# Attention ahead of two gated networks on one core: outer blocks' edge keys side by side, sums on GpSimd, another order of steps

## The chip, the cores and the metric

One core of a Trainium2 chip runs the whole program in one launch. The metric is the device time of an execution in microseconds (us). TensorE is called PE (its weight loads PEld), VectorE DVE, ScalarE ACT, GpSimd POOL, and SyncE, on whose queue nearly all transfers are issued, SP.

## What is computed

```python
def _attn_ref(q_l, k_l, v_l, q_g, k_g, v_g):      # B, H, Sl, D = 4, 8, 512, 64; Sg = 32
    k_all = np.concatenate([k_g, k_l], axis=2)
    v_all = np.concatenate([v_g, v_l], axis=2)
    out_g = np.matmul(sm(scale * np.matmul(q_g, k_all.transpose(0, 1, 3, 2))), v_all)
    mask = np.abs(pos[:, None] - pos[None, :]) <= 32
    s_ll = np.where(mask, scale * np.matmul(q_l, k_l.transpose(0, 1, 3, 2)), -1e9)
    s_lg = scale * np.matmul(q_l, k_g.transpose(0, 1, 3, 2))
    out_l = np.matmul(sm(np.concatenate([s_lg, s_ll], axis=-1)), v_all)
    return np.concatenate([out_g, out_l], axis=2)

x = attention, as (4 * 544, 512)
x = (sigmoid(x @ w_gate) * (x @ w_val)) @ w_out        # 512 -> 1536 -> 512
h = x @ w_in                                           # 512 -> 2048
g = (a0 + a1 h + a2 h^2 + a3 h^3) / (1 + |b0| |h| + |b1| h^2 + 1e-6)
out = g @ w_out2                                       # 2048 -> 512
```

All is float32; `sm` is a softmax over the keys, with 1e-9 added to the sum.

## The kernel before

Attention runs as 16 units, each a batch entry and a pair of heads (`j` = 0, 1, one in each half of the partitions). A unit's 512 local queries are four blocks `c` of 128. A block sees only its own 128 keys and up to 96 edge keys: the 32 global ones and 32 on either side; the first and last block (c = 0 and 3) have one neighbour only, so 64 edge keys and 192 in all where the inner ones have 224 (`KEYS`). For each block and head the steps are:

- `s_mm(u, half)`: scores of two blocks on PE into one of two score buffers (`pairs`); `s_max`: mask, scale and maximum on DVE, into the tile `p`; `s_exp`: exponential and its row sum on ACT; `s_add`, `s_rec`: the sum gets its 1e-9 (a reduction over two columns) and is inverted, on DVE; `s_norm`: the normalisation on POOL, both heads in one instruction.
- `t_mm(u, c)`: four PE transposes (own keys of both heads, then 128 columns with the edge keys of either head) into one of four `banks` of PSUM; `t_out`: one copy of 512 columns out of it, on DVE for c = 0 and 2, on ACT for 1 and 3.
- `v_own`, `v_edge`: products with own and edge values on PE; `x_hi` (ACT), `x_lo` (DVE): the result as two parts; `x_g`, `x_out`: its share of the global queries.

The global queries of two units go together: `g_mm` (PE), `g_max` (DVE), `g_exp` (ACT), `g_rec` (DVE), `g_norm` (POOL), `g_turn` (PE), `e_own` (DVE), `e_edge` (ACT). In between, `w_mag`, `w_bits`, `w_add`, `w_hi` and `w_lo` prepare the first weights of the gated network, which starts with `first(0, 0)`, line 723, when all units are done.

Every engine works through its own list in order. The lists come from the table `STEPS`: each step has a place for unit 0, unit 1, the even and odd units in between, and units 14 and 15; the place of a middle unit is its number plus the table's value, and all steps are issued in the order of these places. The buffers (`Slots`) are taken and given back in that same order: two score buffers, four banks, four tiles of keys, three of queries, values and probabilities. A step that takes a buffer waits for the last use before it.

Of the kernel before, what the change touches and what calls it, by code (L numbers as in the profile page):

```python
# [8 lines left out]
F32 = mybir.dt.float32  # L9
# [27 lines left out]
def tile_of(tok):  # L37
# [19 lines left out]
    ('g_load', (-193.6, None, 4.1758, None, -6.26303, None)),  # L57
# [11 lines left out]
    ('s_norm', 0, 1, (1.15869, 3.05293, 7.0023, 6.88967, 6.8235, 8.84887)),
    ('s_add', 0, (-4.78283, 1.74976, 6.09143, 6.12871, 6.18832, 6.08334)),  # L70
    ('s_rec', 0, (-4.63935, 2.74797, 6.2835, 6.31798, 6.21174, 6.47475)),
    ('s_mm', 1, (-37.43525, -11.09496, 5.07416, 4.48179, 5.14953, 5.5168)),
    ('s_max', 1, 0, (-32.36454, -4.31373, 5.37653, 4.99397, 5.32926, 5.67216)),
    ('s_exp', 1, 0, (-28.29228, 5.29168, 5.84691, 6.27648, 5.63018, 6.75453)),
    ('s_norm', 1, 0, (-19.32734, 6.416, 6.34497, 7.13507, 9.01965, 27.97716)),
    ('s_max', 1, 1, (-26.61698, -6.53723, 5.38946, 5.68801, 5.52636, 5.70039)),
    ('s_exp', 1, 1, (-26.56671, 5.18384, 5.81313, 6.30095, 5.93787, 5.86118)),
    ('s_norm', 1, 1, (1.44586, 6.17569, 7.31762, 7.11427, 7.91441, 11.00704)),
    ('s_add', 1, (-20.31348, 5.90938, 6.14497, 6.64992, 6.09973, 7.27147)),
    ('s_rec', 1, (-19.82663, 6.09145, 6.28248, 6.68668, 6.10739, 8.17753)),  # L80
    ('g_mm', (-27.40611, None, 4.501, None, 4.54575, None)),
    ('g_max', (-26.24706, None, 4.71585, None, 4.64024, None)),
    ('g_exp', (-24.76355, None, 4.94489, None, 5.02262, None)),
    ('g_rec', (-14.86346, None, 5.73461, None, 6.29334, None)),
    ('g_norm', (-14.83861, None, 6.20628, None, 6.92266, None)),
    ('g_turn', (-6.44609, None, 6.70996, None, 6.93773, None)),
    ('e_own', (1.49794, -1.68988, 6.8847, 5.74138, 8.26861, 6.11579)),
    ('e_edge', (2.81072, 2.58086, 7.08973, 6.25701, 8.30143, 6.79597)),
    ('t_mm', 0, (0.8243, 5.9286, 7.28143, 7.79149, 9.41117, 40.10613)),
    ('t_out', 0, (2.43049, 6.10843, 7.68441, 7.94095, 11.87654, 41.58592)),  # L90
    ('v_own', 0, (4.15643, 6.25318, 7.70991, 8.55565, 394.83877, 414.41785)),
    ('v_edge', 0, (4.99735, 6.3075, 7.87462, 8.61583, 395.97761, 414.51208)),
    ('t_mm', 1, (2.22876, 5.75977, 7.19455, 7.68987, 14.15807, 11.38739)),
    ('t_out', 1, (5.28033, 5.92209, 7.49688, 7.80584, 23.59935, 19.86153)),
    ('v_own', 1, (5.89053, 6.83402, 8.18053, 8.61706, 434.20982, 415.84308)),
    ('v_edge', 1, (6.05524, 6.85992, 8.19946, 8.79119, 437.33562, 419.33359)),
    ('t_mm', 2, (-8.43225, 7.73408, 7.32894, 7.95716, 10.57072, 42.59335)),
    ('t_out', 2, (2.42448, 7.97099, 7.75793, 7.99656, 15.45124, 414.50625)),
    ('v_own', 2, (4.32497, 8.69969, 8.00172, 9.00748, 396.7707, 424.89989)),
    ('v_edge', 2, (4.86799, 8.73029, 8.1423, 9.33108, 397.12023, 426.50916)),  # L100
    ('t_mm', 3, (3.98898, 6.97862, 7.32925, 7.65514, 10.38176, 13.58618)),
    ('t_out', 3, (5.43741, 7.38094, 7.82717, 7.77506, 14.15911, 29.43003)),
# [67 lines left out]
def attention(ctx, tc, ident, xh, xl, ins, other):  # L170
# [33 lines left out]
    for t in wn:  # L204
        nc.gpsimd.memset(t[0 : 128 - EDGE], 0.0)
# [1196 lines left out]
```

## Time and profile before

| what | value |
|---|---|
| median of 3 runs | 899.43 us (898.97 to 900.34) |
| profiled execution | 898.83 us, its span 896.9 us |
| PE busy | 889.3 us, 99% of the span |
| DVE, ACT, POOL busy | 750.1, 576.2, 576.0 us |
| granted TensorE clock | 1.0 of full speed in the whole span |
| attention stage | to 114.58 us, when the first gated matmul starts |

Busy time counts an instruction from its start to its end. Matmuls are pipelined and their ends are modelled, so several short matmuls in a row overlap in the profile; how far apart they start tells more than how long one is.

### The profile page before, as it was taken

The numbers are of one execution on the slowest core, as the hardware profiler recorded it, in microseconds if no ns is written. First come the engines' busy times: TensorE is split into PE (matmuls) and PEld (weight loads), VectorE is DVE, ScalarE is ACT, GpSimd is POOL, SyncE is SP. The second block draws the span as 40 slices with busy tenths as digits, with TensorE's granted clock in tenths as the row PEclk, the third lists the DMA queues.
The fourth block names the chain that finished last, engine by engine and source line by source line (L and its number), as shares of the span: only waits on it lengthen the run. The fifth ranks groups of instructions, "written<-read, shape, count | busy, mean of one in ns | idle before, by whom it ended". The sixth has DMA issues, their size and how long they took to land.

```text
span 896.9 us, 13592 instructions
## 1 busy us (share of the span) xinstructions
PE 889.3 (99%) x4592; PEld 737.3 (82%) x4592; DVE 750.1 (84%) x1300; ACT 576.2 (64%) x1161; POOL 576.0 (64%) x470
## 2 busy tenths in 40 slices
PE   8999999999999999999999999999999999999997
PEld 6788988888888888888888888888888888888886
DVE  6999967988889888766868699987788899888886
ACT  6999865445554344354444488777777787777773
POOL 5768765767767485476767767544555676666564
PEclk9999999999999999999999999999999999999999
DMA  9775274767667686999998960022001300110112
GB/s 307 242 219 170 83 280 169 267 227 252 232 236 262 231 300 217 322 339 321 341 352 331 360 213 1 1 94 94 1 1 51 114 24 1 43 51 1 48 59 94
DMA packets 60372, 155.87 MB, mean 174 GB/s; under 512 B 7056, under 2 KB 8720, under 8 KB 60304
## 3 DMA queue, kind: packets, MB, share of 16 engines
q1 hardware_dynamic: 60208, 154.89, 49.7%
q8 instruction: 36, 0.59, 0.3%
q14 instruction: 32, 0.26, 0.1%
q10 hardware_dynamic: 96, 0.13, 0.1%
HBM read 102.83 MB, written 52.17 MB: 173 GB/s over the span
## 4 chain that ended last, share of the span: by engine, by line
PE 87%; DVE 7%; ACT 1%; POOL 1%; issue 0%; POOLq 0%; ACTq 0%
PE rp L1255 6%; PE rp L1257 6%; PE rp L1256 6%; PE rp L725 5%; PE rp L723 5%; PE rp L724 5%; PE p L844 4%; PE p L842 4%; PE p L843 4%; PE pg L723 3%; PE pg L724 3%; PE pg L725 3%; PE pv L723 3%; PE pv L724 3%; PE pv L725 3%; PE pair L265 2%
## 5 line engine op out<-in xcount | busy, mean ns | idle before, releaser
L1172 POOL TENSOR_TENSOR v<-v,u 128x512 f32<-128x512 f32 x68 | 93.4, 1374 | 105.6 <-ACT v L1168 103.4
L1226 POOL TENSOR_TENSOR rgl<-t,rgh 128x512 fp32r<-128x512 f32 x64 | 89.1, 1393 | 40.6 <-POOL v L1172 17.3
L1255 PE MATMUL rp<-wide,rgh 128*128 128x512 f32 x204 | 79.5, 390 | 0.6 <-DVE racc L1276 0.6
L1257 PE MATMUL rp<-wide,rgl 128*128 128x512 f32 x204 | 79.4, 389 | 0.0
L1256 PE MATMUL rp<-wide,rgh 128*128 128x512 f32 x204 | 79.4, 389 | 0.0
L1165 ACT ACTIVATE u<-rp 128x512 f32<-128x512 f32 x68 | 40.5, 596 | 60.2 <-PE rp L725 57.3
L1180 DVE TENSOR_TENSOR t<-rp,t 128x512 f32<-128x512 f32 x68 | 46.7, 687 | 38.7 <-ACT t L1176 37.6
L723 PE MATMUL rp<-yh,wide 128*128 128x512 f32 x192 | 75.0, 391 | 0.0
L1205 DVE SCALAR_TENSOR_TENSOR t<-t,co,v 128x512 f32<-128x512 f32 x68 | 72.9, 1072 | 2.4
L770 ACT CAST gh<-t 128x512 fp32r<-128x512 f32 x38 | 23.6, 620 | 79.7 <-DVE t L763 76.0
L725 PE MATMUL rp<-yh,wide 128*128 128x512 f32 x192 | 74.7, 389 | 0.0
L724 PE MATMUL rp<-yl,wide 128*128 128x512 f32 x192 | 74.7, 389 | 0.0
L1201 DVE SCALAR_TENSOR_TENSOR v<-v,u 128x512 f32<-128x512 f32 x68 | 73.8, 1085 | 0.0
L301 POOL TENSOR_TENSOR p<-p,r 128x384 f32<-128x384 f32 (+1 forms) x64 | 55.4, 889 | 28.4 <-DVE r L295 13.9
L1197 DVE SCALAR_TENSOR_TENSOR v<-v,u 128x512 f32<-128x512 f32 x68 | 61.7, 908 | 1.1 <-ACT u L1193 1.1
L285 ACT ACTIVATE p<-p,mx 128x224 f32<-128x224 f32 (+1 forms) x128 | 58.5, 467 | 6.1 <-DVE mx L277 6.1
L856 DVE TENSOR_TENSOR gacc<-p,gacc 128x512 f32<-128x512 f32 x80 | 51.2, 680 | 10.1 <-PE p L844 10.1
L1168 ACT ACTIVATE v<-u,co 128x512 f32<-128x512 f32 x68 | 55.6, 817 | 2.3
L775 DVE TENSOR_TENSOR gl<-t,gh 128x512 fp32r<-128x512 f32 x38 | 37.4, 985 | 23.1 <-ACT gh L770 23.0
L1189 ACT ACTIVATE u<-v,co 128x512 f32<-128x512 f32 x68 | 49.2, 724 | 6.2 <-POOL v L1172 6.0
L1176 ACT ACTIVATE t<-rp,co 128x512 f32<-128x512 f32 x68 | 51.7, 761 | 0.0
L1214 ACT CAST rgh<-t 128x512 fp32r<-128x512 f32 x64 | 39.1, 611 | 18.0 <-DVE t L1205 18.0
(724 smaller groups left out, 2913.1 us busy)
## 6 DMA issues: line engine op xcount, KB each, us to landing
raw1gv<-in_w_gate_val SPq DMA_DIRECT2D x24, 512.0 KB, 4.2
raw2in<-in_w_in SPq DMA_DIRECT2D x16, 512.0 KB, 5.0
raw2out<-in_w_out SPq DMA_DIRECT2D x16, 512.0 KB, 5.0
kn<-in_k_l SPq DMA_DIRECT2D x15, 448.0 KB, 5.5
raw1out<-in_w_out SPq DMA_DIRECT2D x12, 512.0 KB, 4.2
vn<-in_v_l SPq DMA_DIRECT2D x16, 256.0 KB, 3.2
out<-racc SPq DMA_DIRECT2D x16, 256.0 KB, 2.0
qn<-in_q_l SPq DMA_DIRECT2D x15, 256.0 KB, 4.5
```

Source lines behind the costliest of these rows:

```text
L285: nc.scalar.activation(p, p, AF.Exp, bias=s["mx", half][:, n : n + 1], scale=-1.0, accum_out=s["sm", half][:, n, 0:1])
L723: nc.tensor.matmul(ps, wh, mh[:, k], start=k == 0, stop=False)
L724: nc.tensor.matmul(ps, wh, ml[:, k], start=False, stop=False)
L725: nc.tensor.matmul(ps, wl, mh[:, k], start=False, stop=k == 3)
L1172: nc.gpsimd.tensor_tensor(s["v"], s["v"], s["u"], ALU.mult)
L1197: nc.vector.scalar_tensor_tensor(s["v"], s["v"], Q_CONST, s["u"], ALU.add, ALU.mult)
L1201: nc.vector.scalar_tensor_tensor(s["v"], s["v"], 2.0, s["u"], ALU.subtract, ALU.mult)
L1205: nc.vector.scalar_tensor_tensor(s["t1"], s["t1"], a0, s["v"], ALU.add, ALU.mult)
L1226: nc.gpsimd.tensor_tensor(s["gl"], s["t1"], s["gh"].bitcast(F32), ALU.subtract)
L1255: nc.tensor.matmul(ps, gh[:, w], wh, start=k == 0, stop=False)
L1256: nc.tensor.matmul(ps, gh[:, w], wl, start=False, stop=False)
L1257: nc.tensor.matmul(ps, gl[:, w], wh, start=False, stop=k == G - 1)
```

## The change

In the outer blocks (c = 0 and 3) the two heads' probabilities lie side by side: own keys of head 0, the 64 edge keys of head 0, the 64 of head 1, own keys of head 1. One transpose of the 128 columns in the middle turns the edge keys of both heads, so `t_mm` issues three transposes there and `t_out` copies 384 columns. The edge values of an outer block are laid out in 128 rows, with zeros where the other head's keys stand, so `v_edge` has the same count of matmuls; edge values are loaded as 128 rows for all blocks. Keys lie in 960 columns per unit for 896, with the edge keys of an outer block on both sides of its own keys, and `g_mm` reads the own keys in two pieces of 256 columns. `g_norm` copies the 32 global columns to a second place, and `e_edge` becomes two copies of 64 partitions. `s_add` becomes an addition on POOL. The fills of the edge values and of unused probabilities go; the mask has a third part. All places of the table change from unit 1 on (unit 0 keeps its own).

```diff
+OUTER = (0, NBLK - 1)
+KAT = (0, 256, 256 + WIN, 256 + 2 * WIN, 512 + 2 * WIN)
 STEPS = [
...
-    ('load', 'k', (None, -181.26379, 4.10399, 2.93904, -7.29458, 3.04983)),
-    ('load', 'q', (None, -40.52201, 4.43, 2.15593, 4.42898, -1.01145)),
-    ('load', 'v', (3.92294, -7.4328, 4.44095, 7.56662, 9.81241, 4.88656)),
-    ('load', 'w', (-28.52292, 6.10594, 6.86833, 6.60856, 7.04185, 5.77992)),
+    ('load', 'k', (None, -61.63139, 3.4381, 2.24976, 3.62724, -4.25923)),
+    ('load', 'q', (None, -28.06102, 4.04664, 3.68304, -0.91483, 3.9796)),
+    ('load', 'v', (3.92294, 5.78863, 6.77615, 6.6405, 6.54417, 8.82375)),
+    ('load', 'w', (-28.52292, 5.13391, 6.65689, 7.96598, 332.79805, 9.10943)),
...
-    ('x_out', (397.6786, 9.48477, 15.22727, 12.74181, 508.4924, 477.88016)),
+    ('x_out', (397.6786, 369.83157, 485.83533, 10.26943, 485.83433, 495.48873)),
...
-    kept = dict(kn=slots(one, "kn", 4, [128, NBLK, WIN]), qn=slots(one, "qn", 3, [128, NBLK, 128]),
+    kept = dict(kn=slots(one, "kn", 4, [128, KAT[-1]]), qn=slots(one, "qn", 3, [128, NBLK, 128]),
...
+    def probs(u, c, j):
+        if c in OUTER:
+            return st[u]["p"][:, c].rearrange("p j k -> p (j k)")[:, j * KEYS[c] : (j + 1) * KEYS[c]]
+        return st[u]["p"][:, c, j]
...
-    for t in wn:
-        nc.gpsimd.memset(t[0 : 128 - EDGE], 0.0)
...
-    for t in kept["p"].tiles:
-        for c in (0, NBLK - 1):
-            nc.gpsimd.memset(t[:, c, :, KEYS[c] :], 0.0)
...
-            nc.sync.dma_start(wn[u % 3][128 - EDGE : 128], ins["w_l"][b, pr])
+            nc.sync.dma_start(wn[u % 3], ins["w_l"][b, pr])
...
     def s_add(u, half):
-        nc.vector.tensor_reduce(r, st[u]["sm", half], mybir.AxisListType.X, ALU.add)
+        n = st[u]["sm", half]
+        nc.gpsimd.tensor_tensor(r, n[:, :, 0], n[:, :, 1], ALU.add)
...
     def g_mm(u):
-        for at, n, keys in ((0, S, lambda k: k[:, :, 0:128]), (S, SG, lambda k: k[:, 0, 128:160])):
+        own = lambda k, at, skip, n: k[:, at : at + 2 * n].rearrange("p (c n) -> p c n", n=n)[:, :, skip : skip + 128]
+        for at, n, keys in ((0, 256, lambda k: own(k, 64, 0, KAT[1] - 64)), (256, 256, lambda k: own(k, 384, 96, 64 + WIN)),
+                            (S, SG, lambda k: k[:, 384 : 384 + SG])):
...
     def g_norm(u):
+        copy(pgn[u // 2 % 2][:, S + 64 : S + 64 + SG], n[:, S:])
...
     def e_edge(u):
-        at = 64 * (u % 2)
-        src = st[u - u % 2]["ge"][:, at : at + 64].rearrange("p (h g) -> p h g", h=2)
-        nc.scalar.copy(turned(u)[:, 0, 2:4, 128:160], src)
+        for j in range(2):
+            rows, at = slice(64 * j, 64 * j + 64), 64 * (u % 2) + SG * j
+            nc.scalar.copy(turned(u)[rows, 0, 2, 128:160], st[u - u % 2]["ge"][rows, at : at + SG])
...
     def t_mm(u, c):
         for j in range(2):
-            nc.tensor.transpose(ps[:, 128 * j : 128 * j + 128], s["p"][:, c, j, 0:128], ident)
-        for j in range(2):
-            nc.tensor.transpose(ps[:, 256 + 128 * j : 384 + 128 * j], s["p"][:, c, j, EDGE:WIN], ident)
+            own = probs(u, c, j)[:, KEYS[c] - 128 :] if c in OUTER and j else probs(u, c, j)[:, 0:128]
+            nc.tensor.transpose(ps[:, 128 * j : 128 * j + 128], own, ident)
+        if c in OUTER:
+            nc.tensor.transpose(ps[:, 256:384], s["p"][:, c].rearrange("p j k -> p (j k)")[:, 128:256], ident)
+        else:
+            for j in range(2):
+                nc.tensor.transpose(ps[:, 256 + 128 * j : 384 + 128 * j], s["p"][:, c, j, EDGE:WIN], ident)
...
     def t_out(u, c):
-        src = st[u]["pt", c].rearrange("p (n k) -> p n k", n=4)
-        (nc.scalar.copy if c in T_ACT else nc.vector.tensor_copy)(turned(u)[:, c, :, at : at + 128], src)
+        n = 3 if c in OUTER else 4
+        src = st[u]["pt", c].rearrange("p (n k) -> p n k", n=4)[:, 0:n]
+        (nc.scalar.copy if c in T_ACT else nc.vector.tensor_copy)(turned(u)[:, c, 0:n, at : at + 128], src)
```

The lists that the table gives, in the steady stage, for PE (an even unit e with the odd one o before it; the global queries are those of the next pair), before and after:

```
before  g_mm | t_mm o3 o1 | g_turn | t_mm o0 o2 | s_mm | t_mm e1 e0 e2 e3 | s_mm | v of o and e
after   g_mm | t_mm o3 o1 | g_turn | t_mm o2 o0 | s_mm | t_mm e1 e0 e3 e2 | s_mm | v of o and e
```

SP's list starts, before: keys and queries of unit 0, global queries, keys and queries of unit 1, identity, edge values of unit 0, values of unit 1, a weight, values of unit 0, a weight, queries, keys of unit 3, keys of unit 2, ..., keys of unit 14. After: keys and queries of unit 0, global queries, keys of unit 1, identity, edge values of unit 0, queries of unit 1, a weight, values of unit 0, a weight, keys of units 3 and 2, queries of unit 2, ..., values of unit 1; the keys of unit 14 come with those of the last units.

## Rows read from the trace of the kernel before

**Rows 1.** Page, busy time by engine, and the chain that ended last.

```profile
PE 889.3 (99%) x4592; PEld 737.3 (82%) x4592; DVE 750.1 (84%) x1300; ACT 576.2 (64%) x1161; POOL 576.0 (64%) x470
...
PE 87%; DVE 7%; ACT 1%; POOL 1%; issue 0%; POOLq 0%; ACTq 0%
```

**Rows 2.** Busy time by stretch: from:to, length, each engine's us (instructions), clock, DMA.

```profile
11.14:31.70 20.56, 18.86 (x168) 13.48 (x167) 20.07 (x91) 20.14 (x72) 15.42 (x16) 1.00 0.94 313
...
40.51:53.18 12.67, 12.67 (x143) 11.27 (x142) 11.67 (x61) 11.77 (x45) 8.72 (x11) 1.00 0.61 191
53.18:65.86 12.68, 12.68 (x144) 11.28 (x142) 12.54 (x61) 11.63 (x45) 7.06 (x7) 1.00 0.86 252
65.86:78.55 12.69, 12.69 (x144) 11.27 (x142) 11.70 (x63) 12.08 (x46) 11.43 (x16) 1.00 0.69 220
...
101.10:114.58 13.48, 13.48 (x161) 12.38 (x157) 10.29 (x35) 10.12 (x31) 11.83 (x14) 1.00 0.39 114
114.58:200.00 85.42, 85.42 (x381) 70.67 (x380) 70.18 (x94) 45.61 (x83) 52.88 (x41) 1.00 0.68 239
```

**Rows 3.** Waits, 40.5 to 103.6 us: who for whom, us, times, longest.

```profile
POOL p L301 <- ACT p L285: 12.1, 5, 3.9
...
PEld bank L368 <- POOL p L301: 0.4, 2, 0.2
```

**Rows 4.** PE's waits from 114 us to the end.

```profile
PE rp L1255 <- DVE racc L1276: 0.6, 1, 0.6
PE rt L1221 <- DVE t L1205: 0.2, 1, 0.2
```

**Rows 5.** PE in order of time, steady stage: start, us, operation, tiles.

```profile
56.63 0.38 PE L368 MATMUL bank<-ident,p 128*128 128x128 f32 x2
56.85 0.38 PE L370 MATMUL bank<-ident,p 128*128 128x128 f32 x2
...
63.72 1.11 PE L310 MATMUL pair<-kn,qgn 128*64 128x512 f32 x8
```

**Rows 6.** Groups by line and shape, to 120 us: count, busy us, mean ns, idle before.

```profile
L360 ACT COPY to<-bank 128x64 f32<-128x64 f32 x16 | 2.5, 217 | 0.0
...
L376 DVE COPY to<-bank 128x512 f32<-128x512 f32 x32 | 21.0, 678 | 0.6 <-PE bank L370 0.6
...
L354 DVE COPY to<-bank 128x128 f32<-128x128 f32 x32 | 7.1, 282 | 0.0
...
L291 DVE TENSOR_REDUCE r<-sum 128x4 f32<-128x8 f32 x32 | 4.5, 152 | 0.5 <-ACT p L285 0.5
...
L376 ACT COPY to<-bank 128x512 f32<-128x512 f32 x32 | 17.6, 584 | 2.0 <-ACT p L285 1.0 <-PE bank L370 0.7
```

**Rows 7.** The same view, POOL's groups.

```profile
L301 POOL TENSOR_TENSOR p<-p,r 128x384 f32<-128x384 f32 x32 | 26.5, 827 | 17.7 <-ACT p L285 12.1 <-DVE r L295 3.4 <-PE pair L265 0.8
...
L225 POOL TENSOR_TENSOR xh<-xga,zero 128x128 fp32r<-128x128 f32 x4 | 1.8, 457 | 0.3
...
L208 POOL MEMSET sum<- 128x8 f32 x6 | 0.3, 94 | 0.0
```

**Rows 8.** PE and POOL in order of time, unit 0.

```profile
14.91 0.44 PE L368 MATMUL bank<-ident,p 128*128 128x128 f32 x2 [0.52 <-POOL p L301]
15.80 0.44 PE L368 MATMUL bank<-ident,p 128*128 128x128 f32 x2 [0.24 <-POOL p L301]
...
14.03 2.50 POOL L301 TENSOR_TENSOR p<-p,r 128x384 f32<-128x384 f32 x3 [0.46 <-DVE r L295]
```

**Rows 9.** ACT and PE in order of time, around the tightest place.

```profile
52.78 1.07 ACT L376 COPY to<-bank 128x512 f32<-128x512 f32 x2 [0.21 <-PE bank L370]
...
54.00 0.38 PE L368 MATMUL bank<-ident,p 128*128 128x128 f32 x2
```

**Rows 10.** POOL in order of time, the tail.

```profile
104.48 0.46 POOL L434 TENSOR_TENSOR xga<-xga 128x128 f32<-128x128 f32 x1
...
105.49 0.46 POOL L438 TENSOR_TENSOR xl<-xga,xh 128x128 fp32r<-128x128 f32 x1
...
112.10 1.28 POOL L623 TENSOR_TENSOR wide<-v10gv,wide 128x512 fp32r<-128x512 f32 x1
```

More of the change, by code (lines that the diff above doesn't have):

```diff
@@ L69 @@
[L69 to L90, printed above, removed]
@@ new lines @@
+    ('s_norm', 1, 1, (1.44586, 6.38369, 7.00426, 7.36666, 7.9478, 8.27194)),
+    ('s_add', 1, (-20.31348, 5.32369, 6.61829, 6.53153, 6.66913, 7.55909)),
+    ('s_rec', 1, (-19.82663, 6.0661, 6.81265, 6.90493, 6.74998, 7.60701)),
+    ('g_mm', (-27.40611, None, 4.47309, None, 4.64551, None)),
+    ('g_max', (-26.24706, None, 4.79832, None, 4.69468, None)),
+    ('g_exp', (-24.76355, None, 5.17156, None, 4.98728, None)),
+    ('g_rec', (-14.86346, None, 5.51362, None, 5.41268, None)),
+    ('g_norm', (-14.83861, None, 6.18572, None, 6.20555, None)),
@@ new lines @@
+    ('g_turn', (-6.44609, None, 6.85701, None, 7.58278, None)),
+    ('e_own', (1.49794, -4.33659, 6.98172, 5.94622, 7.8325, 6.91382)),
+    ('e_edge', (2.81072, 2.63581, 7.09372, 6.4148, 10.2212, 7.83107)),
+    ('t_mm', 0, (0.8243, 5.73392, 7.32311, 7.97616, 11.45108, 365.91684)),
+    ('t_out', 0, (2.43049, 6.15028, 7.7834, 8.04351, 17.31224, 374.94186)),
+    ('v_own', 0, (4.15643, 6.41109, 8.12981, 8.93491, 343.06144, 436.712)),
+    ('v_edge', 0, (4.99735, 7.30215, 8.13958, 8.97766, 347.58653, 448.37076)),
@@ new lines @@
+    ('v_edge', 2, (4.86799, 8.68348, 8.33061, 8.73093, 369.80061, 388.2368)),
+    ('t_mm', 3, (3.98898, 6.42779, 7.4158, 7.72771, 334.48592, 353.24455)),
+    ('t_out', 3, (5.43741, 6.87456, 7.65963, 7.81224, 347.58753, 359.29177)),
+    ('v_own', 3, (6.29444, 8.90253, 8.39949, 8.81859, 384.64318, 443.83981)),
+    ('v_edge', 3, (6.41143, 8.92823, 8.41543, 8.96607, 440.99135, 443.86217)),
+    ('x_hi', 0, (6.88716, 7.46028, 8.4693, 9.09131, 379.42546, 480.56602)),
+    ('x_lo', 0, (8.18819, 7.91302, 8.5357, 9.24075, 462.98194, 488.45504)),
@@ L199, in attention @@
     nc.vector.memset(m, 0.0)
-    pgn = [one.tile([128, S + EDGE], F32, name=f"pgn{i}") for i in range(2)]
+    pgn = [one.tile([128, S + 128], F32, name=f"pgn{i}") for i in range(2)]
     wn = [one.tile([128, NBLK, 128], F32, name=f"wn{i}") for i in range(3)]
@@ L264, in s_mm @@
                 rows = slice(64 * j, 64 * j + 64)
-                nc.tensor.matmul(ps[:, j, i * WIN : i * WIN + KEYS[c]], s["qn"][rows, c], s["kn"][rows, c, 0 : KEYS[c]],
+                at, to = KAT[c] + (64 if c in OUTER and j == 0 else 0), i * WIN
+                nc.tensor.matmul(ps[:, j, to : to + KEYS[c]], s["qn"][rows, c], s["kn"][rows, at : at + KEYS[c]],
                                  start=True, stop=True)
@@ L283, in s_exp @@
         for n in (2 * i, 2 * i + 1):
[L284 removed]
+            p = probs(u, 2 * half + i, n % 2)
             nc.scalar.activation(p, p, AF.Exp, bias=s["mx", half][:, n : n + 1], scale=-1.0,
@@ L1369, in laid @@
     own, edge = pairs(x["k_l"], x.pop("k_g"))
-    x["k_l"] = np.concatenate([own, edge], axis=1).transpose(2, 3, 4, 0, 1)
+    out = [edge[c, 0:64] for c in OUTER]
+    k = [out[0], own[0], out[0], own[1], edge[1], own[2], edge[2], out[1], own[3], out[1]]
+    x["k_l"] = np.concatenate(k).transpose(1, 2, 3, 0)
     own, edge = pairs(x["v_l"], x.pop("v_g"))
-    x["v_l"], x["w_l"] = own.transpose(2, 3, 1, 0, 4), edge.transpose(2, 3, 1, 0, 4)
+    w = np.zeros((NBLK, 128) + edge.shape[2:], edge.dtype)
+    for c in range(NBLK):
+        if c in OUTER:
+            for j in range(2):
+                w[c, 64 * j : 64 * j + 64, ..., 64 * j : 64 * j + 64] = edge[c, 0:64, ..., 64 * j : 64 * j + 64]
+        else:
+            w[c, 128 - EDGE :] = edge[c]
+    x["v_l"], x["w_l"] = own.transpose(2, 3, 1, 0, 4), w.transpose(2, 3, 1, 0, 4)
     q = x["q_g"].reshape(B, 2, 2, 2, SG, D)
```

83 lines of the change are left out of this document (45 added, 38 removed).

## The prediction

> **What bounds the kernel now.** I began with the page. TensorE (PE) is busy for 889.3 of 896.9 us and carries 87% of the chain that ended last, VectorE (DVE) 7% [rows 1]. A share over the whole span hides stages, so the second view was busy time in stretches cut at the kernel's own period: from about 31.7 us the attention stage repeats every 12.68 us, one pair of units [rows 2]. Three things are to be seen there. From 11.1 to 31.7 us, the ramp, PE is busy only 18.86 of 20.56 us while DVE and ScalarE (ACT) have 20.07 and 20.14: those two bound it. In each pair PE is busy all the time, with DVE at 11.67 to 12.54 and ACT at 11.63 to 12.08 close behind. From 101.1 to 114.58 us, the tail, PE is again without a gap, and at 114.58 us the first gated layer starts and runs just as full. The third view, the waits of 40.5 to 103.6 us, has the waits on GpSimd (POOL) and a few on ACT; no PE matmul stands in its list, and the weight loads, which run beside the matmuls, waited for POOL's probabilities 0.4 us in two places [rows 3]. After the attention stage PE waits 0.6 us in one place and 0.2 us in another, the larger one for DVE [rows 4]. So the kernel's time is PE's program: whatever moves the start of the first gated layer moves the end by as much, and only PE work or PE waits before 114.58 us count.
>
> **The change part by part.** It is summed against the profiled execution: 898.83 us, of which 896.9 are its span and 1.93 lie around it. The median of the three runs is 0.60 us above it, and I add the same change to both.
>
> *Transposes.* In the blocks c = 0 and 3 of each unit three transposes take the place of four. Groups of two start 0.22 us apart in the steady stage (56.63 and 56.85 us), so one costs 0.11 us [rows 5]. The durations of such rows overlap and are not used. 16 units with two such blocks are 32 x 0.109 = 3.49 us. Four of the blocks belong to units 0 and 1, which run in the ramp, where PE is not the bound; the 28 others give -3.05 us. There is nothing beside PE in this stretch that could hide them. The Trainium skill, TensorE: Matmul & The Clock Gate, section Back-to-back issue gap, has some 81 ns for a matmul of 128 columns in a sustained stream; by it the term would be an estimated -2.3 us and the sum below an estimated -1.8. The row is of these very instructions and longer, so the row decides.
>
> *Scores of the global queries.* The 512 keys are now read in two pieces, so g_mm issues 12 matmul records for 8, over the same columns. Eight records of 512 and 32 columns took 1.11 us [rows 5]. Below, the four more cost nothing, as the columns stay; above, they cost an eighth of that row each, 0.55 us. The columns are the same and PE streams, so I take a value near the lower end, 0.05 us, five times after the ramp: +0.25 us (0 to +2.8).
>
> *Evacuations.* t_out copies 384 columns for 512 in the two outer blocks. On DVE 512 columns took 678 ns and 128 took 282, which is 1.03 ns a column: -0.13 us a unit. On ACT 512 took 584 and 64 took 217, 0.82 ns a column: -0.10 us [rows 6]. e_edge becomes two copies of 32 columns on 64 partitions: one more instruction of at most 217 ns, +0.1 to +0.2 us of ACT. So ACT has the same load as before, within 0.1 us a unit, and DVE less. Neither is on the path unless PE comes too close.
>
> *Sums of the exponentials.* s_add leaves DVE (152 ns, four in a pair, -0.6 us) [rows 6] and becomes a POOL addition of four columns. No row has that. The nearest are a 128-column POOL addition of 457 ns above and a fill of eight columns of 94 ns below [rows 7]; I take 0.2 us, nearer to the fill because there are four columns to add. g_norm gets a 32-column copy, between the same rows, 0.25 us. POOL so has about 1.05 us more per pair; it was busy 7.06 to 11.43 of 12.68 us [rows 2]. The new wait is s_rec's, on DVE, for a POOL addition; all that DVE has queued stands behind it, s_max first, and PE waits for s_max through the two score buffers. POOL's addition itself stands behind normalisations of 827 ns [rows 7]. The work that hides this is the distance from the exponentials to the transposes, of which POOL's long waits for exponentials (12.1 us in five) are a part [rows 3]: it runs dry and refills. I cost it at 0 in the steady stage. The Trainium skill, GPSIMD Engine Reference, section 4.1 Engine selection, speaks against this edit: sums along the free dimension and elementwise additions belong on the Vector engine, GpSimd being some two times slower. The rule concerns the instruction; whether the kernel feels it is the rival POOL below.
>
> *Setup and loads.* Fills of the edge values and of the probabilities go, three mask copies come; both lie ahead of the first scores. Keys grow by 32 KB a unit and edge values by 64 KB. In the steady stage the DMA engines are at 0.61 to 0.86 and take it; in the ramp they are at 0.94, 313 GB/s [rows 2], so the 64 KB more that stand ahead of unit 1's keys make its global scores 0.2 us later. On SP's queue unit 1's queries now stand behind the identity and the edge values, but two score steps and a fill-in of matmuls still lie before their use; the keys of unit 14, which took a key buffer from the seventh unit on, are loaded late, so that unit 4's keys come earlier. I take nothing for both.
>
> *The new order, ramp.* For it: DVE is rid of six additions (-0.5 to -0.9 us) and of 0.13 us in two copies; the exponential step of the global queries of unit 4 stands one local exponential step earlier, and the second half of that unit's scores waited for it. Against it: the transposes of unit 0 are paced by POOL, on which PE waited 0.52 and 0.24 us, with three normalisations in a row of 2.50 us [rows 8]; the copy and two additions now stand between them, +0.65 us, of which DVE's and ACT's own queue hides most by the time of unit 2. With the 0.2 us of the keys I take -0.4 us (-1.2 to +0.9).
>
> *The new order, steady.* PE's list is almost the same: scores, transposes and value products of a pair come in the same blocks, with the outer and inner ones exchanged inside a block. The tightest place before is the pair of transposes that needs the banks of the two ACT copies: copies end at 53.85, PE goes on at 54.00 us [rows 9]. The copy of the outer block, which goes first, gets 0.10 us shorter, PE comes 0.11 us earlier: no change. PE would now need 12.68 - 0.44 = 12.24 us a pair, ACT still 11.63 to 12.08. That is close, so +0.3 us (0 to +1.5).
>
> *The new order, tail.* The global rows of unit 11 (x_out, POOL 104.48 to 105.95 us) now stand ahead of the normalisations of unit 14 and not behind them, and four additions come in between: some 2.3 us more in front of the last transposes [rows 10]. The value products that lie before those cover about two of them: +0.3 us (0 to +1.2). The weights that the first gated layer needs last end on POOL at 113.38 us, 1.2 us before their use [rows 10]; they stand behind the last normalisation and move with it, so I add nothing.
>
> Sum: -3.05 + 0.25 - 0.4 + 0.3 + 0.3 = -2.6 us: 896.2 for an execution like the profiled one, 896.8 for the median.
>
> **The rivals.** *PE gets its time (forecast), 896.8 us.* For it: no PE wait in the steady rows. Its own range is 895.0 to 898.4, from the bounds of ramp, tail and g_mm (its upper end near 0.2 us a time).
>
> *The gain is eaten at the ends, 898.8 us.* PE's work falls, but ramp and tail are set by POOL: ramp +0.7, tail +1.2, g_mm +0.5, -3.05 stays: -0.65. For it: PE's waits for POOL in the ramp [rows 8] and the place of x_out. Against it: DVE, the busiest engine of the ramp, is relieved.
>
> *POOL takes over, 898.1 us.* With additions at the upper row (0.457 us) POOL has 4 x 0.457 + 0.25 = 2.1 us more per pair; in the pair with 11.43 us that is 13.5 us, above 12.24. The pairs with 8.72 and 7.06 take it, so one pair, not all, loses 1.3 us, and the sum is -1.3. The section of the Trainium skill named at the sums would have it go this way. Against it: the normalisations have slack of several microseconds from pair to pair.
>
> *ACT takes over, slower, 901.8 us.* ACT works its list strictly in order, and the new list puts the two x_hi of the odd unit between exponentials, where they wait for the value products; what is queued behind are exponentials. ACT needs 11.65 us of work a pair. Idle time of over 0.6 us a pair makes it the bound, 1.03 us takes the whole gain, and 1.4 us makes a pair 13.05 us, +0.37 in each of 6.5 pairs, +2.4 us. For it: ACT is already at 92 to 95%, and the tightest link [rows 9] is one of its copies. Against it: those idles were about 1 us a pair already, and came from PE being late, not from ACT.
>
> **How the numbers follow.** A measurement of this kernel can tell about 0.2%, 1.8 us, from no change: faster means under 897.6, slower over 901.2 us. Forecast 0.52; ends 0.22; POOL 0.12; ACT 0.14. As faster, within and slower they split into 0.47, 0.05, 0; 0.05, 0.15, 0.02; 0.05, 0.07, 0; and 0, 0.04, 0.10. Together: faster 0.57, same 0.31, slower 0.12. The range takes the lower end of the forecast and reaches over the ends' case up to the foot of ACT's: 894.9 to 900.6 us; beyond lie the rest of ACT's and a ramp that gains over 1.2 us.
>
> **What would show it.** Right: the first gated matmul at about 112 us, pairs of 12.24 to 12.30 us, PE without a gap from about 31 us, three transposes in 0.33 us. g_mm: its span against 1.11 us. Ramp: the first pair's scores of unit 4 by about 0.4 us earlier. Tail: PE waits for POOL's normalisations of units 14 and 15. POOL: waits of transposes for normalisations in the pairs with weight work. ACT: PE waiting for ACT copies, a period over 12.4 us. The prediction is wrong if the period stays at 12.68 us, or if the gated layers, which were full before, do not keep the earlier start.

## The result and the profile after

The changed kernel took 904.49 us (median of 6 runs, 904.03 to 904.92) against 899.2 us before (6 runs, 898.84 to 900.34): a ratio of 1.0058, 95% interval 1.0047 to 1.0068. It is slower by 5.3 us where 2.6 us less was forecast, and lies outside the range. The profiled execution took 904.03 us, its span is 902.2 us.

The page of the changed kernel, busy time by engine, granted clock in 40 slices, and the chain that ended last:

```profile
PE 887.8 (98%) x4592; PEld 736.7 (82%) x4592; DVE 744.1 (82%) x1271; ACT 578.8 (64%) x1177; POOL 581.6 (64%) x501
...
PEclk9999989999999999999999999999999999999999
...
PE 86%; DVE 7%; ACT 3%; DMA 1%; POOL 1%; issue 1%; SPq 0%; POOLq 0%; DVEq 0%; ACTq 0%
```

Beside [rows 1] TensorE is busy 1.5 us less, and the span is 5.3 us longer: time was lost in waiting. Two marks say where. The chain has a share of DMA that it did not have before, and the sixth slice (113 to 135 us) is the only one with a clock below 9 tenths. The waits of TensorE name the transfer (who for whom, us, times, longest):

```profile
PE bank L416 <- DMA wn<-in_w_l: 5.7, 1, 5.7
PE bank L385 <- POOL p L314: 1.3, 2, 0.8
...
PE rp L1276 <- DVE racc L1297: 0.6, 1, 0.6
```

One wait of 5.7 us, for the edge values `wn` of unit 14, is new; the others are small or stood in the kernel before ([rows 4], [rows 8]). TensorE around it in order of time:

```profile
106.48 0.49 PE L407 MATMUL bank<-to,vn 128*64 128x160 f32 x4
112.64 0.80 PE L416 MATMUL bank<-to,wn 128*64 128x160 f32 x4 [5.67 <-DMA wn<-in_w_l]
...
120.19 0.50 PE L744 MATMUL pg<-xh,wide 128*128 128x512 f32 x1
```

The first gated matmul starts at 120.19 us for 114.58 [rows 2], 5.6 us later, and the kernel ends 5.3 us later: the whole loss lies ahead of it. Why the transfer came late stands on SP's queue (issues in order of time, then what the queue waited for):

```profile
98.49 0.38 SPq L242 DMA_DIRECT2D wn<-in_w_l  x1
108.72 0.33 SPq L578 DMA_DIRECT2D raw1gv<-in_w_gate_val  x1
109.10 0.42 SPq L242 DMA_DIRECT2D wn<-in_w_l  x1
...
SPq L578 <- DVE v11gv L607: 9.8, 1, 9.8
```

The seventh weight fetch (`w_next` 6, into `raw1gv`) stands ahead of the load. Its buffer is one of three, and VectorE reads the old content until 108.65 us (L607). The queue stood still behind it for 9.8 us; the load was issued at 109.10 and TensorE went on at 112.64 us. In the table of places this is one number: `('load', 'w', ...)` has 332.79805 for unit 14, where the kernel before had 7.04185, and `w_next` 6 has 41 in both. The queue of the kernel before had the same wait, with nothing behind it that TensorE needed soon:

```profile
100.82 0.83 SPq L236 DMA_DIRECT2D wn<-in_w_l  x2
...
110.80 0.35 SPq L557 DMA_DIRECT2D raw1gv<-in_w_gate_val  x1
...
SPq L557 <- DVE v11gv L586: 8.6, 1, 8.6
```

The wait did not end at 112.64 us. Busy time by stretch of the changed kernel (from:to, length, each engine's us, granted clock, DMA share, GB/s):

```profile
100.00:106.50 6.50, 6.50 (x70) 5.34 (x67) 5.16 (x22) 6.23 (x26) 6.10 (x10) 1.00 0.15 55
106.50:112.60 6.10, 0.47 (x5) 0.17 (x4) 2.11 (x3) 1.39 (x3) 2.86 (x3) 0.84 0.41 132
112.60:118.00 5.40, 5.36 (x36) 4.47 (x38) 1.39 (x3) 1.51 (x4) 0.06 (x1) 0.55 0.01 2
118.00:120.20 2.20, 2.20 (x39) 2.03 (x35) 0.65 (x3) 1.12 (x3) 2.20 (x2) 1.00 0.07 28
```

While TensorE had nothing to do, its granted clock went from 1.00 (2.4 GHz) to 0.50 (1.2 GHz), and most of the work that had waited ran at a mean of 0.55. Shorter stretches have 1.00 up to 110 us, 0.50 from 111 to 117 us and 1.00 again from 118 us on. In the kernel before this stage had 1.00 [rows 2]. The Trainium skill, TensorE: Matmul & The Clock Gate, section Part 1: The HAM clock gate, says that the engine's clock is gated by how busy it has lately been, with half rate as the state of an idle engine; these rows agree (0.84 and 0.55 are stretches that hold both levels).

### The profile page after: what moved, and what is told of

Read it like the earlier page. It is cut to its first block, busy times and chain, and to the rows that moved or that the text cites. A ratio compares the mean times of both kernels' runs of the same rounds, so it can differ in the third digit from the quotient of the medians.

```text
span 902.2 us, 13593 instructions
## 1 busy us (share of the span) xinstructions
PE 887.8 (98%) x4592; PEld 736.7 (82%) x4592; DVE 744.1 (82%) x1271; ACT 578.8 (64%) x1177; POOL 581.6 (64%) x501
## 4 chain that ended last, share of the span: by engine, by line
PE 86%; DVE 7%; ACT 3%; DMA 1%; POOL 1%; issue 1%; SPq 0%; POOLq 0%; DVEq 0%; ACTq 0%
PE rp L1276 6%; PE rp L1278 6%; PE rp L1277 6%; PE rp L744 5%; PE rp L746 5%; PE rp L745 5%; PE p L865 4%; PE p L863 4%; PE p L864 4%; PE pg L744 3%; PE pg L745 3%; PE pg L746 3%; PE pv L744 3%; PE pv L745 3%; PE pv L746 3%; PE pair L274 2%
## 5 line engine op out<-in xcount | busy, mean ns | idle before, releaser
L1186 ACT ACTIVATE u<-rp 128x512 f32<-128x512 f32 x68 | 40.5, 596 | 60.7 <-PE rp L746 57.8
L294 ACT ACTIVATE p<-p,mx 128x192 f32<-128x192 f32 (+1 forms) x128 | 58.5, 462 | 5.3 <-DVE mx L286 5.1
L1205 DVE SCALAR_TENSOR_TENSOR t<-t,co,rp 128x512 f32<-128x512 f32 x68 | 50.2, 738 | 0.0
```

Of the source, the lines that this page charges most:

```text
L294: nc.scalar.activation(p, p, AF.Exp, bias=s["mx", half][:, n : n + 1], scale=-1.0, accum_out=s["sm", half][:, n, 0:1])
```

## The experiments

My theory: the queue. The load stood behind an entry that waits, which cost 5.7 us, and the clock that fell in the wake of the wait cost 2 to 3 us more; all else went about as forecast. The rivals: the load is late for another reason (its place, its size), the ends of the attention stage would have eaten the gain in any case, or the clock's fall has no weight. All ratios below are against the kernel before on the same chip. Its median there was 899.01 us for e1 to e4, 899.20 for e5 to e8, and 898.98 for e9 to e11; a difference between runs of two of these groups is taken with each run against its own.

**The load ahead of the fetch** (e1), and **the fetch behind the load** (e2), each one number of the changed kernel's table:

```diff
-    ('load', 'w', (-28.52292, 5.13391, 6.65689, 7.96598, 332.79805, 9.10943)),
+    ('load', 'w', (-28.52292, 5.13391, 6.65689, 7.96598, 6.65689, 9.10943)),     # e1
-    ('w_next', 6, (41.0,)),
+    ('w_next', 6, (347.5,)),                                                     # e2
```

> The changed kernel with one number other: the load of unit 14's edge values gets the place 20.66 of its neighbours' pattern (14 + 6.65689) for 346.80 (14 + 332.79805), so that on SP's queue it stands ahead of the seventh weight fetch and not behind it. Theory (queue): the whole loss is one TensorE wait of 5.7 us at 106.5 us for this load, which stood behind a fetch that waits for a buffer that VectorE frees only at 108.65 us, and the TensorE clock that fell to 1.2 GHz for 6.8 us in its wake. About 5.0 us of full-speed TensorE work is left at 106.5 us, so the first gated matmul starts at about 111.5 us (120.2 in the changed kernel, 114.6 before), no wait of over 0.5 us before it, granted clock 1.00: 896.1 us (895.6 to 896.8), ratio to before 0.9966. Rival (ends): the new order's tail waits for GpSimd as well and the load only hid it; then a wait for GpSimd's normalisations of units 14 and 15 of 1 to 3 us appears in the same place and the time is 897.5 to 900. Rival (late load as such, or a larger transfer): the load is late whatever stands ahead of it, time stays near 904.5.

> The changed kernel with the other of the two transfers moved: the seventh weight fetch goes behind the load of unit 14's edge values (place 347.5 for 41), and the load keeps its late place. Theory (queue): what is late is not the load's place but the entry ahead of it; the load is issued as soon as the edge buffer is free, about 101 us as in the kernel before, and the time is that of the run in which the load goes ahead, 896.1 us (895.6 to 896.8), while the fetch still waits for VectorE to about 108.7 us without cost. Rival (late load as such): the load is issued after 108 us again, TensorE waits about 5.7 us at 106.5 us, 904.5 us. Rival (ends): 897.5 to 900 with a wait for GpSimd.

Measured: e1 896.96 us, ratio 0.9976 (0.9968 to 0.9985); e2 896.83 us, ratio 0.9976 (0.9966 to 0.9985). SP's queue in e2:

```profile
100.28 0.86 SPq L242 DMA_DIRECT2D wn<-in_w_l  x2
110.53 0.33 SPq L578 DMA_DIRECT2D raw1gv<-in_w_gate_val  x1
```

TensorE's only listed wait from 85 to 130 us is one of 0.4 us (e1) and 0.3 us (e2), for GpSimd's `x_out`. Either number alone turns a loss of 5.3 us into a gain of 2.1; in e2 the load kept its late place. So it was the entry ahead of it, not its place or its size, and the rival of the ends is out as the cause of the loss. Both medians are a little above what was expected, and the profiled executions tell why: the first gated matmul came at 113.64 us (e1), not at 111.5, mainly because the clock fell in another place, in the ramp (e5 below, without that fall, has 112.28). Stretches of e1:

```profile
14.00:16.00 2.00, 0.77 (x5) 0.54 (x6) 2.00 (x10) 1.93 (x7) 2.00 (x4) 1.00 1.05 390
16.00:18.00 2.00, 1.87 (x15) 1.40 (x15) 1.97 (x5) 1.98 (x5) 2.00 (x3) 0.79 1.06 396
18.00:20.00 2.00, 2.00 (x20) 1.89 (x18) 1.97 (x3) 1.91 (x9) 2.00 (x2) 0.50 1.03 409
```

Of the 20 executions of e1 and e2, 10 had a mean clock of 0.999 or 1.00 and took 895.9 to 896.9 us; 10 had 0.997 or 0.998 and took 897.0 to 898.1.

**The move alone, in the kernel before** (e3):

```diff
-    ('load', 'w', (-28.52292, 6.10594, 6.86833, 6.60856, 7.04185, 5.77992)),
+    ('load', 'w', (-28.52292, 6.10594, 6.86833, 6.60856, 332.79805, 5.77992)),
```

> The kernel before with nothing of the change but this one move: its load of unit 14's edge values goes behind the seventh weight fetch (place 346.80 for 21.04). Theory (queue): the fetch waits there for the buffer that VectorE frees at about 110.8 us, the load is issued after it and lands 3.5 to 4 us later, about 114.5 us; the first value product with unit 14's edges, due near 110 us, waits 4 to 5 us, and the clock falls for some microseconds as in the changed kernel, 2 to 3 us more: 905 to 907 us, ratio 1.007 to 1.009. Rival (the move costs nothing by itself and it is the change's order that makes the wait): within 0.2% of 899.2 us, no wait for this load.

Measured: 906.23 us, ratio 1.0081 (1.0068 to 1.0094), as the queue's theory had it. TensorE in e3:

```profile
115.63 0.80 PE L395 MATMUL bank<-to,wn 128*64 128x160 f32 x4 [5.05 <-DMA wn<-in_w_l]
...
121.32 0.50 PE L723 MATMUL pg<-xh,wide 128*128 128x512 f32 x1
```

One number makes the kernel before 7.2 us slower: a wait of 5.05 us, and a first gated matmul 6.7 us later than in [rows 2]. The move needs nothing else of the change to do its harm.

**The price of the clock** (e4 with 56 matmuls, e8 with 24), in the changed kernel:

```diff
     def v_edge(u, c):
         s = st[u]
+        if (u, c) == (14, 0):
+            for _ in range(56):          # e8: 24
+                nc.tensor.matmul(pairs.tiles[0][:, 0, 0:128], still, still, start=True, stop=True)
```

> The changed kernel plus 56 matmuls of a zero tile with itself (128 columns each, some 0.107 us, 6.0 us in all) on TensorE right ahead of the product that waits for unit 14's edge values; they compute nothing that is used. TensorE so works through the time in which it waited. Theory (the clock is a part of the loss): the granted clock stays at 1.00, the last 5 us of attention run at full speed, and the first gated matmul starts at about 117.7 us for 120.2: 902.0 us (901.4 to 902.6), so that of the 8.7 us lost 2.5 to 3 are the clock's. Rival (the clock in the trace's wake is without weight, the work after the wait was bound by something else): the same 904.5 us, within 0.5.

> The changed kernel (load of unit 14's edge values in its late place) plus 24 matmuls of the zero tile with itself ahead of the product that waits for that load: 24 x 0.228 = 5.5 us of work in a wait of 5.7 us. The 56 of the run before turned out to be 0.228 us each, 12.8 us in all, so its total says nothing by itself; behind them TensorE's clock was 1.00 and the work up to the first gated matmul took 5.30 us, against 7.55 us in the changed kernel. Theory (the clock is 2.25 us of the loss): the wait ends as before at about 112.7 us, the first gated matmul starts at about 118.0 us for 120.2, 902.3 us (901.8 to 903.0). Rival (without weight): 904.5 us within 0.5.

Measured: e4 909.19 us (ratio 1.0115, 1.0100 to 1.0131); e8 903.08 us (1.0043, 1.0029 to 1.0056). In e4 I had mis-sized the filling: each such matmul shows as two records, and 56 of them took 12.8 us. TensorE in e4, then in e8:

```profile
107.40 12.77 PE L415 MATMUL pair<-still 128*128 128x128 f32 x112
120.10 0.49 PE L419 MATMUL bank<-to,wn 128*64 128x160 f32 x4
...
125.40 0.50 PE L747 MATMUL pg<-xh,wide 128*128 128x512 f32 x1
```

```profile
112.73 0.49 PE L419 MATMUL bank<-to,wn 128*64 128x160 f32 x4 [0.25 <-DMA wn<-in_w_l]
...
118.03 0.50 PE L747 MATMUL pg<-xh,wide 128*128 128x512 f32 x1
```

From the product that had waited to the first gated matmul it is 125.40 - 120.10 = 118.03 - 112.73 = 5.30 us in both, and 120.19 - 112.64 = 7.55 us in the changed kernel. The same work cost 2.25 us more at the lower clock. In e8 that product starts within 0.1 us of the changed kernel's and the profiled execution took 901.82 us, 2.2 us less than the changed kernel's; the median gives 1.4, as three of its five executions had a mean clock of 0.998 and took 903.1 to 904.3 us; where their clock fell, no trace shows. Now the loss adds up: 5.67 + 2.25 = 7.9 us lost, 5.6 us later at the first gated matmul, so some 2.3 us had been gained on the way.

**The gaps in the ramp filled** (e5): e1, and in `t_mm`

```diff
+        for _ in range({0: 3, 1: 2}.get(c, 0) if u == 0 else 0):
+            nc.tensor.matmul(ps[:, 384:512], still, still, start=True, stop=True)
```

> The changed kernel with the load of unit 14's edge values at place 20.66, ahead of the seventh weight fetch, plus five matmuls of a zero tile with itself (0.228 us each by the run with 56 of them) in two gaps of the ramp: three ahead of the transposes of unit 0's block 0, two ahead of those of block 1, where TensorE waited 0.83 and 0.50 us for GpSimd's normalisations. They compute nothing that is used. In the profiled runs with the moved load or the moved fetch the granted clock fell to 1.2 GHz at about 16.5 us, behind those gaps, for some 4 us, and half of their executions lie at 897.3 to 898.1 us with a mean clock of 0.997, the others at 895.9 to 896.9 with 1.00. Theory (the gaps bring the clock down in some executions): with the gaps filled the clock holds at 1.00 in all, median 896.1 us (895.8 to 896.8), none above 897.2, first gated matmul at about 112.0 us. Rival (the clock falls there for another reason): two groups as before, median 896.9. Rival (the fill delays the transposes): +0.2 to +0.5 us, median 896.5 with one group.

Measured: 896.25 us (895.82 to 896.89), ratio 0.9965 (0.9953 to 0.9978), the fastest of all, 2.95 us under before. TensorE in e5:

```profile
13.83 0.83 PE L384 MATMUL bank<-still 128*128 128x128 f32 x6
14.83 0.44 PE L387 MATMUL bank<-ident,p 128*128 128x128 f32 x2 [0.16 <-POOL p L314]
...
112.28 0.50 PE L746 MATMUL pg<-xh,wide 128*128 128x512 f32 x1
```

All 38 executions of the changed layout with this fill (e5, e6, e7, e11) had a mean clock of 0.999 or 1.00; e1 and e2 had it in 10 of 20. The chip does not explain this: e8, without the fill and on the chip of e5, has 0.998 in three of five. Not every kernel without the fill has the ramp's fall: the six executions of the changed kernel have 0.996, and the fall behind the long wait accounts for that by itself. With the fill it came in none. Whether it takes work in these two gaps, or more TensorE work anywhere in the ramp would do, no run separates.

**One part taken back at a time.** e6, e7, e10 and e11 have the load ahead and the fill; e9 has the load ahead by its old table, and no fill. e6 puts the sums back on VectorE, e7 adds a fourth transpose to the outer blocks, e10 is the kernel before with the new table:

```diff
-        nc.gpsimd.tensor_tensor(r, n[:, :, 0], n[:, :, 1], ALU.add)
+        nc.vector.tensor_reduce(r, n, mybir.AxisListType.X, ALU.add)                                            # e6
             nc.tensor.transpose(ps[:, 256:384], s["p"][:, c].rearrange("p j k -> p (j k)")[:, 128:256], ident)
+            nc.tensor.transpose(ps[:, 384:512], s["p"][:, c].rearrange("p j k -> p (j k)")[:, 128:256], ident)  # e7
```

> The run with the load moved ahead and the two ramp gaps filled (e5), but the sums of the exponentials completed on VectorE as in the kernel before (32 reductions of 0.152 us there for 32 additions of 0.21 us on GpSimd). Theory (the place of these sums is off the path): VectorE has 0.6 us a pair more, about 11.6 of 12.25 us, and GpSimd 0.8 less; steady pairs stay at 12.25 us and the ramp, where VectorE is full, loses up to 0.5 us: the time of e5, +0 to +0.5 us. Rival (GpSimd takes over): if GpSimd's additions cost the kernel something, this run is faster than e5 by up to 1 us. Rival (VectorE would be the bound without the move): pairs longer than 12.4 us, over +1 us.

> The run with the load moved ahead and the two ramp gaps filled (e5), with a fourth transpose in every outer block again (the third one once more, into the unused quarter of the bank), 32 more of 128 columns. Theory (each costs its 0.109 us on the path wherever TensorE is full): +28 x 0.109 = +3.05 us, four more in the ramp at nothing to 0.4: e5 + 2.9 to 3.5 us, 899.0 to 899.6, steady pairs 12.68 us. Rival (the pair is set by VectorE or ScalarE too, so a part of the transposes is hidden): e5 + 0.5 to 2 us.

> The kernel before (four transposes, sums on VectorE) with the changed kernel's table of places, its load of unit 14's edge values moved ahead of the seventh weight fetch, and the five filling matmuls in the ramp. Theory (the order by itself is worth little): its ramp gains up to 0.9 us, its steady pairs are 12.68 us or a little longer, as VectorE has the sums, and the tail gives back 0.3: 898.5 to 899.6 us, between -0.7 and +0.4 us of before. Rival (the order is the larger part of the gain): 897.5 us or less. Rival (the order was made for the shorter VectorE list and loses without it): 900 us or more, pairs of 12.8 us or longer.

Measured, all in the new order:

| | sums on VectorE | sums on GpSimd |
|---|---|---|
| four transposes | e10: 899.2 us, 1.0005 (0.9996 to 1.0013) | e7: 898.1 us, 0.9987 (0.9979 to 0.9996) |
| three transposes | e6: 898.15 us, 0.9986 (0.9978 to 0.9995) | e5: 896.25 us, 0.9965 (0.9953 to 0.9978) |

The order alone is worth nothing that can be told from no change. The upper row holds two layouts: e10 has that of the kernel before, with copies of 512 columns, and e7 the new one. Taken each against its own kernel before, the transposes (with the layout) bring 1.3 us with the sums on VectorE, and 1.85 with them on GpSimd, not 3.05; the sums bring 1.3 (with the layout) and 1.9. So in e6 and in e7 a rival came true, not the theory. Of the 1.9 us of e6, 0.36 lies outside the span (2.15 us around it, for 1.79 in e5) and 1.1 ahead of the first gated matmul (113.38 for 112.28 us in the profiled executions). The start of the global scores in the steady stage shows how, e5 first, then e6, then e7:

```profile
37.48 1.12 PE L325 MATMUL pair<-kn,qgn 128*64 128x256 f32 x12
49.92 1.12 PE L325 MATMUL pair<-kn,qgn 128*64 128x256 f32 x12
62.17 1.12 PE L325 MATMUL pair<-kn,qgn 128*64 128x256 f32 x12
74.43 1.12 PE L325 MATMUL pair<-kn,qgn 128*64 128x256 f32 x12
86.75 1.12 PE L325 MATMUL pair<-kn,qgn 128*64 128x256 f32 x12
```

```profile
37.60 1.12 PE L325 MATMUL pair<-kn,qgn 128*64 128x256 f32 x12
50.30 1.12 PE L325 MATMUL pair<-kn,qgn 128*64 128x256 f32 x12
62.55 1.12 PE L325 MATMUL pair<-kn,qgn 128*64 128x256 f32 x12
75.22 1.12 PE L325 MATMUL pair<-kn,qgn 128*64 128x256 f32 x12
87.70 1.12 PE L325 MATMUL pair<-kn,qgn 128*64 128x256 f32 x12
```

```profile
37.35 1.12 PE L325 MATMUL pair<-kn,qgn 128*64 128x256 f32 x12
50.03 1.12 PE L325 MATMUL pair<-kn,qgn 128*64 128x256 f32 x12
...
88.08 1.12 PE L325 MATMUL pair<-kn,qgn 128*64 128x256 f32 x12
```

In e7 every pair is 12.68 us. In e5 two of four are 12.25, shorter by four transposes at 0.109 us, as forecast; the others are 12.44 and 12.32. In e6 the pairs are 12.70, 12.25, 12.67 and 12.48: with the sums on VectorE two of four do not get shorter at all, and in the first of them the two blocks of score matmuls take 1.79 and 1.75 us from start to start, for 1.61 and 1.66 in e5. They share two score buffers that VectorE's `s_max` sets free. The weight loads of these matmuls waited for it more often than in e5 (37 to 90 us, e5 first, then e6), and in e10 TensorE itself waited for VectorE, at the sum of L291:

```profile
PEld pair L274 <- DVE mx L286: 0.7, 4, 0.2
```

```profile
PEld pair L274 <- DVE mx L286: 1.2, 6, 0.2
```

```profile
64.04 1.17 PE L310 MATMUL pair<-kn,qgn 128*64 128x512 f32 x8 [0.42 <-DVE r L291]
```

This points to VectorE coming too late for the score buffers. It is not shown to be all: the weight loads waited 0.5 us more, and the four pairs are 0.83 us longer. Nor is it VectorE's load as such: the pair of e6 in which VectorE is fullest, 12.15 of 12.25 us, kept its length, and the two long ones have 11.65 and 11.35.

**The old order with the other two parts** (e9), the changed kernel with the whole `STEPS` table of before:

> The changed kernel with the table of places of the kernel before: three transposes and the sums on GpSimd stay, the order of all steps is the old one (and with it the load of unit 14's edge values ahead of the seventh weight fetch). Theory (the shorter TensorE work and the relieved VectorE carry the gain, the order adds little): 1.6 to 2.9 us under before, 896.3 to 897.6 us, steady pairs 12.25 to 12.40 us. Rival (the order is needed for the shorter pairs, since in the old list the additions on GpSimd or the copies on ScalarE come at the wrong place): pairs of 12.5 us or longer, 898 us or more. Rival (the new order alone gained in the ramp): scores of unit 4 at 29.8 us as before, not at 28.8.

Measured: 901.97 us, ratio 1.0032 (1.0020 to 1.0044). Both my theory and its bounds were wrong, and the rival that the order is needed came true. TensorE's waits to 130 us in e9:

```profile
PE bank L385 <- POOL p L314: 3.1, 5, 0.8
PE bank L358 <- POOL pgn L351: 1.3, 2, 0.7
...
PE bank L385 <- DVE xl L440: 1.0, 2, 0.8
PE pair L274 <- ACT pgn L340: 0.9, 1, 0.9
PE pair L325 <- DVE xga L448: 0.7, 1, 0.7
```

The first two pairs take 13.1 and 13.2 us (the next two 12.4 and 12.5), and the tail has five waits of 0.47 to 0.82 us, 3.45 us in all; the first gated matmul comes at 118.08 us. The new layout needs the new order, although that order by itself gains nothing.

**The global rows back at their old place** (e11), e5 with

```diff
-    ('x_out', (397.6786, 369.83157, 485.83533, 10.26943, 485.83433, 495.48873)),
+    ('x_out', (397.6786, 369.83157, 485.83533, 12.74181, 485.83433, 495.48873)),
```

> The run with the load moved ahead and the ramp gaps filled (e5) with the global rows of the odd units back at the kernel before's place (12.74 for 10.27 behind the unit), so that unit 11's three GpSimd operations stand behind the normalisations of unit 14 again. In e5 TensorE waited 0.32 us at 99.7 us for them. Theory (the tail's price is this wait): it goes, first gated matmul at 112.0 us for 112.28, 895.9 us for 896.25, -0.3 us. Rival (the wait goes on to the normalisations of unit 15, three operations later, or its place is covered): no change within 0.3, or up to +0.5 us.

Measured: 898.49 us, ratio 0.9993 (0.9985 to 1.0002), 2.5 us worse than e5 when each is taken against its own kernel before, and outside all that was expected. The wait of 0.32 us went, and three for GpSimd's normalisations came, at 99.0, 100.7 and 111.1 us:

```profile
PE bank L387 <- POOL p L314: 2.5, 4, 1.5
```

In front of the normalisations of unit 14 these three operations cost 0.3 us. In e11 they stand ahead of the last normalisation of unit 15, where TensorE has nothing left to do meanwhile: the wait at 111.1 us is 1.48 us. The two earlier ones, 0.19 and 0.69 us, go with unit 7: the edit moves the `x_out` of all odd units, unit 7's three operations now run at 94.45 to 95.92 us (at 80.5 in e5), and the normalisations behind them, for which TensorE waits, start at 97.25 us for 95.46. A further 0.35 us went in the four steady pairs (49.62 us for 49.27).

## Why the prediction was wrong, point by point

**The step that failed** is the last sentence of "Setup and loads": "I take nothing for both". It followed the queries of unit 1 and the keys of unit 14 on SP's queue. The edge values of unit 14 move on the same queue, from ahead of the seventh weight fetch to behind it, and that move was neither named nor priced, nor does the list of SP's order ahead of the prediction have it; nor was the wait of the entry that it was moved past. Both were to be had from the kernel before. The fetch waited 8.6 us for VectorE and was issued at 110.80 us; even with the forecast's 2.6 us taken off it would go out at 108.2, and a load behind it would land 3.5 us later (what the loads around it took), at 111.7. All products of the attention stage were to be over at 112: those with unit 14's edges could not be. In place of that nothing the runs showed a wait of 5.67 us for this load and 2.25 us of work at the lower clock behind it. e1, e2 and e3 show that it was this and nothing else. None of the rivals was of this kind: each had an engine as the one that comes too late, and none a transfer.

**The clock** was no term of the sum. The wait cost 2.25 us more than its length (e4, e8).

**What the sum says without this step.** It forecast the first gated matmul at about 112 us, and 896.8 us for the median. e5, which has the whole change with the load ahead and the ramp filled, has 112.28 and 896.25. The total was right to 0.6 us, and that was partly luck: its parts were not, which the stretches tell. The forecast's -3.05 us of transposes are split at 0.109 us each: two blocks, those of unit 2, up to the global scores of unit 6, sixteen in the four steady pairs, ten behind. (One of the five 0.05 us of the global scores lies outside the stretches.)

| stretch | forecast | e5 |
|---|---|---|
| to the global scores of unit 6 (38.32 us before) | -0.22 - 0.4 = -0.62 | 37.48 - 38.32 = -0.84 |
| four steady pairs (50.78 us before) | -1.74 + 0.5 (g_mm, new order) = -1.24 | 49.27 - 50.78 = -1.51 |
| from there to the first gated matmul (25.48 us before) | -1.09 + 0.3 = -0.79 | 25.53 - 25.48 = +0.05 |

Ramp and pairs gained 0.5 us more than forecast, the tail lost 0.84 more. The range that the prediction gives to its forecast case by itself, 895.0 to 898.4 us, does not follow from the bounds named for it: added up, they give 895.5 to 899.8.

- *Transposes.* The price of one held: a group of three takes 0.33 us to the next start, and a pair of e7 is 0.43 us longer than the short ones of e5, for four. That 28 of them lie on the path did not: taking the 32 back costs 1.85 us, and 1.98 at the first gated matmul (114.26 for 112.28). By stretch that is nothing up to unit 6 (37.35 for 37.48), 1.46 of 1.74 us in the pairs, and 0.65 of 1.09 behind them. The forecast's "nothing beside PE that could hide them" failed most in the tail, where TensorE's shorter list met GpSimd (0.32 us at 99.7 us); the rest there is not explained.
- *Scores of the global queries.* +0.25 was too much: twelve records take 1.12 us for 1.11 [rows 5], so +0.0.
- *Sums of the exponentials.* The price was right, 0.214 us on GpSimd by its group's mean for the 0.2 taken. The value was wrong: I wrote that VectorE is not on the path "unless PE comes too close" and gave its relief nothing. It is worth 1.3 us with four transposes and 1.9 with three. VectorE had 11.67 to 12.54 us of a pair's 12.68 [rows 2], and a pair that was to become 12.24 us long left it little room; which of its steps then came late, e6 and e10 only point to. The Trainium skill, GPSIMD Engine Reference, section 4.1 Engine selection, advises VectorE for such additions; by the instruction the trace agrees in the direction (0.214 against 0.152 us, [rows 6], 1.4 times), by the kernel e5 and e6 say the contrary.
- *New order, ramp.* The ramp gained more than -0.4, and not by the order alone: up to the global scores of unit 6, e10 with the order is 0.24 us ahead of before (38.08 us), e6 with the new layout too 0.72 (37.60), e7 with the sums on GpSimd and all transposes 0.97 (37.35). The term hid a danger: GpSimd's normalisations pace the transposes of unit 0 more than before (TensorE's waits 0.83 and 0.50 us, for 0.52 and 0.24 in [rows 8]), and in e1 and e2 the clock fell behind them in half of the executions.
- *New order, steady and tail.* ScalarE did not become the bound: no row of TensorE's waits names its copies, though it is busy 11.90 to 12.33 us in e5's pairs of 12.25 to 12.44. The tail costs more than +0.3: with four transposes it takes 26.18 us (e7) and 26.09 us (e10) for 25.48. I held `x_out` ahead of unit 14's normalisations for a cost; e11 shows that the new places of `x_out` are better by 2.5 us, and e9 that the old list as a whole is worse by 5.9 us with the new layout. The parts are not a sum: the order alone gives 0, with it the transposes or the sums about -1 each, both in the new order -3, both in the old order +3.

## What to carry to other kernels

When a step is moved, list for its queue every entry that it is moved past and ask of each whether it waits for something, and until when: the trace before shows how long such an entry stood, and a load behind it cannot go out sooner. A unit that is relieved is worth nothing only as long as the bound stays where it is; if another part of the change shortens the bound, the place of each step on the engines close behind it becomes a term of the sum. Where TensorE stands still for some microseconds, add to the wait what the work behind it costs at the lower clock, and where a wait cannot be removed, idle matmuls in the gap give that part back.

## What the runs showed of the hardware

- In the wait of 5.67 us TensorE's granted clock fell from 1.00 to 0.50, and the work behind it took 7.55 us for 5.30.
- Two gaps of 0.83 and 0.50 us close to one another in the ramp were followed by a fall of the clock to 0.50 at about 16.5 us in some executions and not in others. The profiled executions of the changed kernel and of e2 both had TensorE busy 0.91 us of the stretch of 14 to 16 us; the clock of the first stayed at 1.00, that of the second fell to 0.55 in the next 2 us. No execution of the kernel before or of e5 shows it. What decides stays open. Such a dip cost 0.9 us by the two groups of e1 (896.68 and 897.53 us) and 1.7 us by those of e2 (895.96 and 897.63).
- A matmul of 128 columns in full precision with a zero tile shows as two records and took 0.228 us (56 in 12.77 us), about twice the 0.109 us between transposes of the same shape.
- A fourth buffer for the fetches, which might take the queue's wait away without touching any order, was not tried.
